# Holding back two weight transfers behind matrix-unit work in the late steps of an attention, router and feed-forward kernel

## The chip, the cores and the metric

The kernel runs on one core of a Trainium2 chip. A core has five engines with a queue of instructions each: PE (matrix products; PEld is its loading of the stationary operand), DVE, ACT, POOL, and SP, which here does nothing but issue DMA transfers, one after the other in the order in which the program wrote them. Sixteen DMA engines move the bytes of every transfer. The metric is the time of one execution in microseconds (us). All of the times below are of the whole kernel unless a stretch is named.

## The reference

Three layers follow each other, all in 32-bit floats (the third's weights come as 64-bit floats in memory and are narrowed in the kernel where they do).

```python
# 1: attention, 4 batches x 8 heads x 576 positions x 64, a causal window of 64
scores = where(0 <= i - j < 64, q @ k.T / 8, -1e9)
attn = softmax(scores)
x = (attn @ v) reshaped to 2304 x 512
# 2: soft mixture of 8 experts with 4 slots each
logits = x @ phi                                # 2304 x 32
slot_input = softmax(logits, over tokens).T @ x # 32 x 512
slot_out[e] = relu(slot_input[e] @ w1[e]) @ w2[e]  # w1: 8 x 512 x 1024, w2: 8 x 1024 x 512
x = softmax(logits, over slots) @ slot_out      # 2304 x 512
# 3: feed-forward
h = x @ w_in                                    # 512 x 2048
out = (h * sigmoid(1.702 h)) @ w_out            # 2048 x 512
```

## The kernel before

**Stages.** Attention comes first, in 18 steps (`for i in range(ns)`): 16 units (a batch and two heads, positions 0 to 511) and 2 steps for the last 64 positions of all batches. The steps overlap: step i does the scores of unit i (`emit_s`, L313 and L328), the turning of the probabilities of unit i-1 (`emit_t`, L348), the turning of the finished rows of unit i-2 (`xt_step`, four 128x128 transposes as PE products, L401), and the product with v of unit i-1 (`emit_pv`, L363). The router's work is spread over the steps. Behind the loop come a short tail of attention and router, then the first expert layer (`emit_w1`, L792), the second (`emit_w2`, L834, and its last pieces, L901), and from about 141 us on the third layer, which is one dense run of PE products (L1014 and L1046).

**Transfers.** The two expert weights are 16 slices of w1 and 16 of w2, of 1 MB each (`plan`). `load_w(n)` takes the next n slices off the plan and writes their transfers into SP's queue (L146). `W_AT` says how many at which step: one at each of the steps 2 to 11, 13 and 14, two at 15, two at 16, three at 17; the rest come behind the loop, as places in SBUF come free (`wslot`, and `dslot` in the attention's own memory, `arena`). Beside them stand the loads of q and k (`load_qk`, L226, of the last positions L228) and of v (`load_v`, L240), written 2 or 3 steps ahead of their use. `AHEAD` (steps 10 to 15) puts a step's slices between its `load_qk` and its `load_v`; otherwise they stand behind both.

**What sets the order.** Each engine does its instructions in the order of the program. A transfer in SP's queue has to wait for its own conditions, and all behind it wait with it: for the reader of the old contents of its place, and for one of eight semaphores that the transfers use in turn (so a transfer waits for the landing of the eighth before it). The slices that the change touches have numbers 10 (step 13), and 14 and 15, the last two of w1 (step 16). Slices 16 to 18, the first three of w2, are those of step 17. The first reader of slices 14 and 15 is the last round of `emit_w1`.

Of the kernel before, what the change touches and what calls it, by code (L numbers as in the profile page):

```python
# [31 lines left out]
HALVES = (slice(0, 256), slice(256, 512))  # L32
LAST_CUT = (slice(0, 384), slice(384, 512))
PIECES = (slice(0, 2), slice(2, 3), slice(3, 4))
W_AT = {**{i: 1 for i in range(2, 17)}, 12: 0, 15: 2, 16: 2, 17: 3}
L_AT = 12
AHEAD = range(10, 16)

# [31 lines left out]
def attention_softmoe_ffn(  # L70
# [12 lines left out]
    nc = tc.nc  # L83
# [21 lines left out]
    def bank(tag, shape=(128, 512), dtype=F32):  # L105
        ring = rings[tag]
        ring.append(ring.pop(0))
        return psp.tile(list(shape), dtype, tag=f"b{ring[-1]}", name=tag)

    ident = cst.tile([128, 128], F32, name="ident")  # L110
# [14 lines left out]
    def wslot(dtype=F32):  # L125
        return wp.tile([128, 4, 512], dtype, tag="w", name="w")

    def dslot(i):
        return mem(2048 * i, 2048).rearrange("p (a f) -> p a f", a=4)
# [3 lines left out]
    plan += [(w2t, w2, i, i if i < 7 else None) for i in range(16)]  # L133
    plan.reverse()

    def load_w(n=1):
        for _ in range(n):
            if plan:
                lst, src, i, d = plan.pop()
                t = wslot() if d is None else dslot(d)  # L140
                v = src[i].rearrange("p (a f) -> p a f", a=4)
                if not plan:
                    t, v = [x.rearrange("p a f -> p (a f)").rearrange(
                        "p (c a f) -> p c a f", c=4, a=4) for x in (t, v)]
                for c in PIECES if not plan else (slice(0, 4),):
                    nc.sync.dma_start(out=t[:, c], in_=v[:, c])  # L146
                lst.append(t)


# [92 lines left out]
    def set_ones(n):  # L242
        v = vbuf(n)
        nc.gpsimd.memset(bass.AP(v.tensor, v.offset, [v.ap[0], [129, 5]]), 1.0)
# [58 lines left out]
    def emit_s(i):  # L303
        u, t = work[i]
        st = [bank("m" if i == 1 and h else "s", (128, 4, 128)) for h in range(2)]
        rows = [slice(64 * h, 64 * h + 64) for h in range(2)]
        for h in range(2):
            for j in range(2):
                o = st[h][rows[j]]
                m = mask[rows[h], j]  # L310
                if t is not None:
                    m = mask[rows[h], 0, 1:2].to_broadcast([64, 4, 128])
                nc.tensor.matmul(  # L313
                    o, identb[rows[h], rows[h]], m,
                    start=True, stop=False, tile_position=(64 * h, 64 * j))
        for c in range(4):
            for h in range(2):
                for j in range(2):
                    r = rows[h]
                    if t is None:  # L320
                        b = qbuf(u)[r]
                        q = b[:, 64 * (2 * c + j):64 * (2 * c + j) + 64]
                        o = c - 1 if c and not j else c
                        k = two(b, 512 + 64 * c, 768 + 64 * o)
                    else:
                        b = qbuf(NU + 2 * t + j)[r, 192 * c:192 * c + 192]
                        q, k = b[:, 0:64], b[:, 64:192]
                    nc.tensor.matmul(  # L328
                        st[h][rows[j], c, :], q, k, start=False, stop=(c == 3),
                        tile_position=(64 * h, 64 * j))  # L330
        nm = sp.tile([128, 2, 4], F32, tag="nm", name="nm")
        for h in range(2):
            nc.vector.tensor_reduce(  # L333
                out=nm[:, h], in_=st[h], axis=AX.X, op=ALU.max, negate=True)
        est[i] = st, nm

    def emit_e(i, h):
        st, nm = est[i]
        for c in range(4):
            nc.scalar.activation(  # L340
                out=pb[h][:, c, :], in_=st[h][:, c, :], func=ACTF.Exp,
                bias=nm[:, h, c:c + 1], scale=1.0)

    def emit_t(i):
        for h in range(2):
            tt = bank("m", (128, 4, 128))
            for c in range(4):
                nc.tensor.transpose(tt[:, c, :], pb[h][:, c, :], ident)  # L348
            nc.scalar.copy(ab[h], tt)  # L349
# [37 lines left out]
    run = {"m": None, "s": None, "acc": None}  # L387

    def xt_step(i, split=False):
        u, t = work[i]  # L390
        pt = bank("m")
        ps = [pt[:, c] for c in HALVES]
        if split:
            ps[1] = bank("m")[:, HALVES[0]]
        for k in range(4):
            if t is None:
                b, kk = divmod(u, NHP)
                src = xb[b % 2][:, k, kk * 128:kk * 128 + 128]
            else:
                src = xl[:, t, k * 128:k * 128 + 128]  # L400
            nc.tensor.transpose(ps[k // 2][:, 128 * (k % 2):128 * (k % 2) + 128], src, ident)  # L401

        def evac():
            if t is None:
                nc.scalar.copy(xT[:, kk], pt)
                return
            o = xlT[:, :, 128 * t:128 * t + 128]
            if not split:
                nc.scalar.copy(o, pt.rearrange("p (k n) -> p k n", k=KD))
                return  # L410
            for k, copy in ((0, nc.scalar.copy), (2, nc.vector.tensor_copy)):
                copy(o[:, k:k + 2], ps[k // 2].rearrange("p (k n) -> p k n", k=2))
        return evac
# [156 lines left out]
    for b in range(B):  # L570
        g = routing(b)
        logits, lmax, dexp, turn, total, slots, gather, norm, side = g
        n = NHP * b
# [25 lines left out]
    def convert(i, first):  # L599
        if not wide:  # L600
            return
        for k in range(5):
            n = CONV_AT.get(i - k)
            if n is None:
                continue
            if k > 1 and first:
                narrow_b(early_raw(n), early_dst(n), (k - 2,))
            elif k == 0 and not first:
                narrow_a(early_raw(n), early_dst(n))
            elif k == 1 and not first:  # L610
                narrow_c(early_dst(n), nc.gpsimd)

    for i in range(ns):
        if i != 2:
            emit_s(i)
        if i:
            emit_t(i - 1)
        for f in lgt.get(i, ()):
            f()
        for f in mid.get(i, ()):  # L620
            f()
        emit_e(i, 0)
        for f in post2.get(i, ()):
            f()
        convert(i, True)
        if i > 1:
            xt_step(i - 2)()
        for f in early.get(i, ()):
            f()
        if i == 1:  # L630
            scale_q(2, nc.vector)
            emit_s(2)
        if i:
            emit_pv(i - 1)
        emit_e(i, 1)
        for f in late.get(i, ()):
            f()
        if i:
            emit_norm(i - 1)
        for f in post.get(i, ()):  # L640
            f()
        if i == 0:
            make_i4()
        if i == 1:
            nc.vector.tensor_copy(
                phi4.rearrange("p k (j s) -> p k j s", j=4),
                phis.unsqueeze(2).to_broadcast([128, KD, 4, NS]))
        if 1 < i < NU - 1:
            scale_q(i + 1, nc.gpsimd)
        for n in {NU - 3: (NU,), NU - 1: (NU + 1,), NU: (NU + 2, NU + 3)}.get(i, ()):  # L650
            scale_q(n, nc.gpsimd)
        if 0 < i < NU:
            set_ones(i)
            shift_v(i)
        elif i >= NU:
            for n in range(2):
                set_ones(NU + 2 * (i - NU) + n)
        if i == L_AT:
            load_qk(NU)
            load_v(NU)  # L660
        if i < NU:
            load_qk(i + 3 + (i + 3 >= NU))
        if i in AHEAD:
            load_w(W_AT.get(i, 0))
        if i < NU + 1:
            load_v(i + 2 + (i + 2 >= NU))
        if i < 2:
            for n in range(2 * i + 2, min(2 * i + 4, FP + N_WO)):
                early_load(n)
        convert(i, False)  # L670
        if i not in AHEAD:
            load_w(W_AT.get(i, 0))

    rings.update(s=[0, 1], t=[2, 7], v=rings["v"])
    cts[0] = s1.tile([128, 1536], F32R, tag="pa", name="cT")
# [7 lines left out]
        out=ml[:, 128:160], in_=pm[0:1, 0:128].rearrange("p (t s) -> p s t", t=TM), axis=AX.X,  # L683
# [12 lines left out]
    def tail_logits(t):  # L696
# [9 lines left out]
    xt = xt_step(ns - 1, True)  # L706
    nc.vector.tensor_scalar(
        out=mm[:, 2:3], in0=pm[:, 0:1], scalar1=-1.0, scalar2=None, op0=ALU.mult)
# [15 lines left out]
        out=ltt, in_=lpt, func=ACTF.Exp, bias=m, scale=1.0, accum_out=ss)  # L724
# [14 lines left out]
    for c in range(2):  # L739
# [9 lines left out]
        out=rsl, in0=pm[:, 0:1], scalar1=ss, scalar2=1e-9, op0=ALU.add, op1=ALU.add)  # L749
# [3 lines left out]
        out=i4s, in0=i4m[:, 0:NS], scalar1=rsl, scalar2=None, op0=ALU.mult)  # L753
    nc.vector.scalar_tensor_tensor(
        out=acc, in0=psl, scalar=al, in1=acc, op0=ALU.mult, op1=ALU.add)
# [479 lines left out]
```

## Time and profile before

| | |
|---|---|
| runs | 362.8, 363.66, 367.47 us; median 363.66 |
| the profiled execution | 362.31 us, its span 360.5 us |
| PE | busy 351.4 us, 97% of the span |
| DVE, ACT, POOL | 67%, 54%, 13% |
| DMA | 70.87 MB, mean 197 GB/s over the span |
| TensorE's granted clock | 1.00 throughout |

The span is cut into 40 slices of 9 us in the page's second part: a digit there is the busy share of an engine, or of the sixteen DMA engines, in tenths. The chain is the row of work that ended last, followed back from the last instruction. "Issue" is time in which an engine waited for nothing that the profile shows. A transfer has two times: the time of its issue on SP, and from there to landing.

### The profile page before, as it was taken

The page shows a single profiled execution, that of the slowest core. Times are in us where ns is not written, and L with a number is a line of the kernel's source. Part 1 is how long each engine was busy: PE and PEld are TensorE (multiplying, and loading weights), DVE is VectorE, ACT ScalarE, POOL GpSimd, SP SyncE. Part 2 cuts the span into 40 slices and gives each one's busy share as a digit, 9 for nine tenths or more (in the row PEclk, how much of TensorE's full clock was granted, in tenths as well). Part 3 has the DMA queues.
Part 4 walks back from the last instruction along what each step waited for, and adds up shares of the span by engine and source line. Part 5 has one row for each costly group of instructions (what it writes and reads, how often), then busy time and mean ns, then how long its engine had stood idle before and what let it go on. Part 6 is the DMA issues. An engine that isn't in the chain of part 4 may idle for free.

```text
span 360.5 us, 7741 instructions
## 1 busy us (share of the span) xinstructions
PE 351.4 (97%) x3021; PEld 269.9 (75%) x3021; DVE 240.5 (67%) x527; ACT 195.6 (54%) x499; POOL 45.5 (13%) x90
## 2 busy tenths in 40 slices
PE   7999999998999999999999999999999999999995
PEld 6787787776634357888788887788886888888884
DVE  4666797976626228885867695988687876262624
ACT  2898899777314026765657444554455453333330
POOL 4366764630100000000000000000000000000000
PEclk9999999999999999999999999999999999999999
DMA  7999999999999994233131313140300000040404
GB/s 278 407 414 405 409 407 413 402 404 407 418 418 422 418 402 150 101 121 113 60 116 58 119 57 119 32 137 9 116 2 0 0 2 1 0 176 0 175 2 175
DMA packets 18180, 70.87 MB, mean 197 GB/s; under 512 B 2016, under 2 KB 2400, under 8 KB 14176
## 3 DMA queue, kind: packets, MB, share of 16 engines
q1 hardware_dynamic: 18000, 70.18, 50.3%
q8 instruction: 24, 0.39, 0.4%
q10 hardware_dynamic: 144, 0.20, 0.2%
q14 instruction: 12, 0.10, 0.1%
HBM read 65.65 MB, written 4.72 MB: 195 GB/s over the span
## 4 chain that ended last, share of the span: by engine, by line
PE 86%; DMA 9%; ACT 2%; issue 1%; DVE 1%; DVEq 0%; ACTq 0%
PE s L1046 18%; PE t L1046 18%; PE v L1046 18%; DMA w<-in_w_dram 8%; PE v L363 5%; PE m L1014 5%; PE m L348 5%; PE s L328 4%; PE s L313 2%; PE m L401 2%; ACT pa L340 2%; PE m L442 1%; PE m L492 1%; DMA rawt<-in_qk_dram 1%; PE m L928 1%
## 5 line engine op out<-in xcount | busy, mean ns | idle before, releaser
L1002 ACT ACTIVATE r<-m 128x384 fp32r<-128x384 f32 (+1 forms) x97 | 47.4, 491 | 80.6 <-PE m L1014 80.5
L1027 DVE TENSOR_TENSOR r<-g,r 128x384 fp32r<-128x384 f32 x96 | 51.4, 554 | 48.4 <-ACT g L1002 40.0
L1046 PE MATMUL t<-w,r 128*128 128x512 f32 x288 | 75.8, 395 | 0.0
L1046 PE MATMUL s<-w,r 128*128 128x512 f32 x288 | 74.3, 392 | 0.0
L1046 PE MATMUL v<-w,r 128*128 128x512 f32 (+2 forms) x291 | 73.4, 387 | 0.0
L1046 PEld LDWEIGHTS t<-w,r 128*128 128x128 f32 x288 | 53.8, 188 | 14.8 <-issue 4.0
L1046 PEld LDWEIGHTS v<-w,r 128*128 128x128 f32 x291 | 54.5, 188 | 11.3
L1046 PEld LDWEIGHTS s<-w,r 128*128 128x128 f32 x288 | 52.6, 188 | 8.5
L1002 ACT ACTIVATE g<-m 128x384 f32<-128x384 f32 x96 | 47.8, 499 | 0.0
L340 ACT ACTIVATE pa<-s,nm 128x128 f32<-128x128 f32 x140 | 41.0, 404 | 5.6 <-DVE nm L333 5.6
L333 DVE TENSOR_REDUCE nm<-s 128x4 f32<-128x512 f32 x35 | 22.5, 684 | 5.5 <-PE s L328 4.8
L1014 PE MATMUL m<-cT,w 128*128 128x384 f32 (+2 forms) x113 | 25.9, 320 | 0.0
L1014 PEld LDWEIGHTS m<-cT,w 128*128 128x128 f32 x113 | 20.8, 188 | 4.9 <-ACT g L1002 0.7
L348 PE MATMUL m<-ident,pa 128*128 128x128 f32 x144 | 20.9, 283 | 0.8 <-ACT pa L340 0.4
L348 PEld LDWEIGHTS m<-ident,pa 128*128 128x128 f32 x144 | 15.6, 140 | 5.0 <-PE s L328 1.7
L349 ACT COPY pa<-m 128x512 f32<-128x512 f32 x18 | 10.7, 596 | 10.2 <-PE m L348 10.2
L982 ACT CAST w<-wf 128x512 fp32r<-128x512 f32 x15 | 9.3, 623 | 9.3 <-DVE wf L176 9.3
L792 PE MATMUL s<-w,phis 128*32 128x512 f32 x128 | 14.1, 594 | 0.0
L382 DVE TENSOR_TENSOR arena<-v,rs 128x256 f32<-128x256 f32 x36 | 13.6, 420 | 0.6
L328 PE MATMUL s<-arena 64*64 64x128 f32 x352 | 13.8, 271 | 0.1
L985 DVE TENSOR_TENSOR w<-wf,w 128x512 fp32r<-128x512 f32 x15 | 10.3, 689 | 5.2 <-ACT w L982 4.9
L1066 DVE TENSOR_TENSOR w<-s,w 128x512 f32<-128x512 f32 x18 | 11.6, 684 | 2.8 <-PE s L1046 2.8
(218 smaller groups left out, 453.3 us busy)
## 6 DMA issues: line engine op xcount, KB each, us to landing
w<-in_w_dram SPq DMA_DIRECT2D x24, 1024.0 KB, 9.9
w<-in_w_out_dram SPq DMA_DIRECT2D x16, 512.0 KB, 3.4
arena<-in_w_dram SPq DMA_DIRECT2D x7, 1024.0 KB, 11.4
iraw<-in_w_in_dram SPq DMA_DIRECT2D x12, 512.0 KB, 3.3
arena<-in_qk_dram SPq DMA_DIRECT2D x10, 512.0 KB, 8.8
out_dram<-w SPq DMA_DIRECT2D x16, 256.0 KB, 2.1
arena<-in_vt_dram SPq DMA_DIRECT2D x13, 258.5 KB, 7.3
rawt<-in_qk_dram SPq DMA_DIRECT2D x6, 512.0 KB, 8.7
```

The source lines that it names most:

```text
L328: nc.tensor.matmul(st[h][rows[j], c, :], q, k, start=False, stop=(c == 3), tile_position=(64 * h, 64 * j))
L333: nc.vector.tensor_reduce(out=nm[:, h], in_=st[h], axis=AX.X, op=ALU.max, negate=True)
L340: nc.scalar.activation(out=pb[h][:, c, :], in_=st[h][:, c, :], func=ACTF.Exp, bias=nm[:, h, c:c + 1], scale=1.0)
L348: nc.tensor.transpose(tt[:, c, :], pb[h][:, c, :], ident)
L363: nc.tensor.matmul(pvt[i][h][64 * j:64 * j + 64, c, :], ab[h][:, c, 64 * j:64 * j + 64], v, start=True, stop=True, tile_position=(0, 64 * j))
L382: nc.vector.tensor_tensor(out=o, in0=pv[h][:, :, 1 - h:65 - h], in1=rs[:, h].unsqueeze(2).to_broadcast([128, 4, 64]), op=ALU.mult)
L792: nc.tensor.matmul(ph[32 * j:32 * j + 32, :], siT[:, kk, :], w1t[4 * r + kk][:, j, :], start=(kk == 0), stop=(kk == KD - 1), tile_position ...
L1002: nc.scalar.activation(out=(gh, g)[part][:, a:e], in_=ph[:, a:e], func=ACTF.Gelu_apprx_sigmoid)
L1014: nc.tensor.matmul(ph[:, c - a:e - a], mst[:, f * 128:f * 128 + 128], cT(c, e - c), start=True, stop=True)
L1027: nc.vector.tensor_tensor(out=gl, in0=g, in1=gh.bitcast(F32), op=ALU.subtract)
L1046: nc.tensor.matmul(accs[t][:, h], a[:, c], b[:, h], start=(first and k == 0), stop=(last and k == 2 and h.stop == 512))
L1066: nc.vector.tensor_tensor(out=o[:, h], in0=accs[t][:, h], in1=o[:, h], op=ALU.add)
```

## The change

Three things are changed, all of them in the transfers of weight slices. `xt_step` keeps its last transposing product in `run["xt"]`. In the steps named in `BEHIND` (13 and 17) `load_w` gets that product and gives the first transfer that it issues a wait for it (`add_manual_dep`). And `W_AT` moves the two slices of step 16 to step 17, which now issues five.

```diff
-W_AT = {**{i: 1 for i in range(2, 17)}, 12: 0, 15: 2, 16: 2, 17: 3}
+W_AT = {**{i: 1 for i in range(2, 17)}, 12: 0, 15: 2, 16: 0, 17: 5}
+BEHIND = (13, 17)
...
+    behind = {}
+
+    def start_w(out, in_):
+        x = nc.sync.dma_start(out=out, in_=in_)
+        if behind:
+            tc.add_manual_dep(x.ins, behind.pop("pe").ins.name, mybir.DependencyInfo(
+                mybir.DependencyClass.Sync, mybir.DependencyReason.DATA), reason="behind")
+
-    def load_w(n=1):
+    def load_w(n=1, pe=None):
+        if pe is not None:
+            behind["pe"] = pe
...
-                    nc.sync.dma_start(out=t[:, c], in_=v[:, c])
+                    start_w(out=t[:, c], in_=v[:, c])
...
-            nc.tensor.transpose(ps[k // 2][:, 128 * (k % 2):128 * (k % 2) + 128], src, ident)
+            run["xt"] = nc.tensor.transpose(
+                ps[k // 2][:, 128 * (k % 2):128 * (k % 2) + 128], src, ident)
...
         if i in AHEAD:
-            load_w(W_AT.get(i, 0))
+            load_w(W_AT.get(i, 0), run["xt"] if i in BEHIND else None)
...
         if i not in AHEAD:
-            load_w(W_AT.get(i, 0))
+            load_w(W_AT.get(i, 0), run["xt"] if i in BEHIND else None)
```

SP's queue around step 13, before the change (behind each transfer the semaphores that it waits for; DMAHW0 to 7 are the eight of the transfers):

```order
L226 DMA rawt<-in_qk_dram 128x1024 [waits DMAHW7_49,PE_49,Pool_49]
L240 DMA arena<-in_vt_dram 128x517 [waits DMAHW0_49,PE_49,Pool_49]
L228 DMA arena<-in_sq_dram 128x768 [waits DMAHW1_49,PE_49,Pool_49]
L146 DMA w<-in_w_dram 128x2048 [waits DMAHW2_49]
L240 DMA rawt<-in_vt_dram 128x517 [waits DMAHW3_49,PE_49,Pool_49]
```

and with the change:

```order
L237 DMA rawt<-in_qk_dram 128x1024 [waits DMAHW7_49,PE_49,Pool_49]
L251 DMA arena<-in_vt_dram 128x517 [waits DMAHW0_49,PE_49,Pool_49]
L239 DMA arena<-in_sq_dram 128x768 [waits DMAHW1_49,PE_49,Pool_49]
L140 DMA w<-in_w_dram 128x2048 [waits DMAHW2_49,PE_49]
L251 DMA rawt<-in_vt_dram 128x517 [waits DMAHW3_49,PE_49,Pool_49]
```

Nothing changes its place; the slice in the fourth row waits for PE now.

SP's queue from the two slices of step 15 to the three of step 17, before the change (the last two transfers of v are those of the steps 15 and 16):

```order
L146 DMA w<-in_w_dram 128x2048 [waits DMAHW0_49]
L146 DMA w<-in_w_dram 128x2048 [waits DMAHW1_49,DVE_49,Activation_49]
L240 DMA arena<-in_vt_dram 128x517 [waits DMAHW2_49,PE_49,Pool_49]
L240 DMA rawt<-in_vt_dram 128x517 [waits DMAHW3_49,PE_49,Pool_49]
L146 DMA w<-in_w_dram 128x2048 [waits DMAHW4_49,DVE_49,Activation_49]
L146 DMA w<-in_w_dram 128x2048 [waits DMAHW5_49,DVE_49,Activation_49]
L146 DMA arena<-in_w_dram 128x2048 [waits DMAHW6_49]
L146 DMA arena<-in_w_dram 128x2048 [waits DMAHW7_49,PE_49,Pool_49]
L146 DMA arena<-in_w_dram 128x2048 [waits DMAHW0_49,PE_49,Activation_49]
```

and with the change:

```order
L140 DMA w<-in_w_dram 128x2048 [waits DMAHW0_49]
L140 DMA w<-in_w_dram 128x2048 [waits DMAHW1_49,DVE_49,Activation_49]
L251 DMA arena<-in_vt_dram 128x517 [waits DMAHW2_49,PE_49,Pool_49]
L251 DMA rawt<-in_vt_dram 128x517 [waits DMAHW3_49,PE_49,Pool_49]
L140 DMA w<-in_w_dram 128x2048 [waits DVE_49,DMAHW4_49,PE_49,Activation_49]
L140 DMA w<-in_w_dram 128x2048 [waits DMAHW5_49,DVE_49,Activation_49]
L140 DMA arena<-in_w_dram 128x2048 [waits DMAHW6_49]
L140 DMA arena<-in_w_dram 128x2048 [waits DMAHW7_49,Pool_49]
L140 DMA arena<-in_w_dram 128x2048 [waits DMAHW0_49,PE_49,Activation_49]
```

Here too the order stays: step 16 wrote nothing into SP's queue behind its two slices. The fifth row (slice 14) waits for PE now, and the eighth (slice 17) no longer does, since the fifth ahead of it has waited for a later point of PE. PE, DVE, ACT and POOL have the same instructions in the same order.

## Rows read from the trace of the kernel before

**Rows 1.** The page's second part: DMA share in tenths and GB/s, 40 slices.

```profile
DMA  7999999999999994233131313140300000040404
GB/s 278 407 414 405 409 407 413 402 404 407 418 418 422 418 402 150 101 121 113 60 116 58 119 57 119 32 137 9 116 2 0 0 2 1 0 176 0 175 2 175
```

**Rows 2.** Busy time by stretch: engines, then clock, DMA share, GB/s.

```profile
84.00:88.00 4.00, 4.00 (x79) 3.23 (x79) 2.57 (x12) 4.00 (x13) 0.21 (x2) 1.00 1.02 416
88.00:131.00 43.00, 40.88 (x409) 18.46 (x408) 18.59 (x53) 10.90 (x26) 1.83 (x1) 1.00 1.01 416
131.00:138.00 7.00, 6.88 (x47) 4.84 (x40) 4.71 (x11) 4.58 (x12) 0.00 (x0) 1.00 0.91 349
141.00:355.00 214.00, 214.00 (x978) 175.32 (x977) 147.81 (x269) 107.25 (x241) 0.00 (x0) 1.00 0.19 65
```

**Rows 3.** The chain that ended last: start, us, what.

```profile
88.67 1.16 issue
...
99.58 2.76 PE s L792 x24
...
102.35 13.34 DMA w<-in_w_dram
...
115.71 15.08 DMA w<-in_w_dram
...
130.84 0.43 PE v L901 x8
```

**Rows 4.** SP in order of time: start of issue, us, transfer.

```profile
63.02 0.33 SPq L228 DMA_DIRECT2D arena<-in_sq_dram  x1
63.39 0.43 SPq L146 DMA_DIRECT2D w<-in_w_dram  x1
65.49 0.33 SPq L240 DMA_DIRECT2D rawt<-in_vt_dram  x1
...
80.47 0.33 SPq L240 DMA_DIRECT2D rawt<-in_vt_dram  x1
80.91 0.85 SPq L146 DMA_DIRECT2D w<-in_w_dram  x2
81.80 15.31 SPq L146 DMA_DIRECT2D arena<-in_w_dram  x7
100.63 15.40 SPq L146 DMA_DIRECT2D w<-in_w_dram  x11
```

**Rows 5.** DMA issues between 80.4 and 81.3: KB, us to landing.

```profile
w<-in_w_dram SPq DMA_DIRECT2D x1, 1024.0 KB, 7.3
rawt<-in_vt_dram SPq DMA_DIRECT2D x1, 258.5 KB, 5.2
```

**Rows 6.** DMA issues between 62.9 and 63.3.

```profile
arena<-in_sq_dram SPq DMA_DIRECT2D x1, 384.0 KB, 7.9
```

**Rows 7.** Transfers of 512 KB at 136 to 165, on L151: count, last line all seven.

```profile
L151 SPq DMA_DIRECT2D iraw<-in_w_in_dram x4: 327/327/328, 152.3 to 164.2; - x4
L151 SPq DMA_DIRECT2D w<-in_w_out_dram x3: 327/328/328, 136.6 to 147.2; - x3
...
DMA to landing us min/median/max: 3.1/3.3/3.7
```

**Rows 8.** PE in step 17, in order of time.

```profile
83.50 0.60 PE L401 MATMUL m<-ident,arena 128*128 128x128 f32 x4
84.03 0.69 PE L363 MATMUL v<-arena,pa 128*64 128x65 f32 x15
```

**Rows 9.** PE in step 13, in order of time.

```profile
61.81 1.04 PE L328 MATMUL s<-arena 64*64 64x128 f32 x32
...
63.71 0.60 PE L401 MATMUL m<-ident,arena 128*128 128x128 f32 x4
...
64.75 0.64 PE L363 MATMUL v<-rawt,pl 128*64 128x65 f32 x16
```

## The prediction

> **What bounds the kernel now.** I read the page's slices first, then the busy times by stretch, then the chain, and last SP's queue with the landings.
>
> The slices show two kernels in one [rows 1]. For the first 15 slices of 9 us, up to about 135 us, the DMA engines are busy to nine tenths or more (the first slice apart) and move some 410 GB/s; after that they are mostly idle. The stretches say the same more sharply [rows 2]: from 88 to 131 us the DMA share is 1.01 at 416 GB/s, from 141 to 355 us it is 0.19 and PE is busy 214.00 of 214 us. PE is also nearly always busy before 131 us, but that is no bound there, and the chain shows why [rows 3]: behind 2.76 us of the first expert layer it runs through two transfers of weight slices, 13.34 us from 102.35 and 15.08 us from 115.71, and only at 130.8 us is PE on it again. So two stages decide: **a stream of transfers that ends at 130.8 us, and then PE**. What delays the stream's last byte delays all behind it by as much, since PE from 141 us on has no idle time to give back [rows 2].
>
> The stream is a queue. Transfers land in the order of their issue, and each waits for those ahead. The v load of 80.47 us needs 5.2 us to land at 85.7, and the slice of 80.91 us needs 7.3 and lands at 88.2 [rows 4, 5]: 2.5 us later, which is what 1 MB takes at 416 GB/s (1.049 MB / 416 = 2.52 us). A transfer's late issue therefore costs nothing as long as its predecessors still keep the DMA engines busy when its own first bytes are ready.
>
> **Step 13.** One slice waits newly for the transposes of `xt_step`. They end at 63.71 + 0.60 = 64.31 us [rows 9]; SP issued the slice at 63.39 [rows 4]. What SP needs from a PE end to an issue I take from the rows: the scores end at 62.85 and the q and k load that waits for them goes at 63.02, 0.17 us; the product with v ends at 65.39 and its load goes at 65.49, 0.10 us [rows 4, 9]. So the slice goes at about 64.45, 1.05 us later. Cover: the transfer just ahead, issued at 63.02, lands 7.9 us later, at 70.9 [rows 4, 6], so 6.5 us of queue still stand before the slice. Cost 0. Behind the slice in SP's queue stands the v load, which goes at 65.49 because of PE [rows 4]; the slice's issue takes 0.43 us, so SP is free again at 64.9 and the load is not late. Cost 0.
>
> **Step 17.** Slices 14 and 15 went at 80.91 and, right behind it, 81.4; slice 16, first of the step's own three, at 81.80 [rows 4]. Now slice 14 waits for the transposes, which end at 83.50 + 0.60 = 84.10 [rows 8]. With 0.10 to 0.17 us for SP it goes at 84.2, **3.3 us later**. The four behind it follow at SP's pace, 0.85 us for two [rows 4], so about 84.7, 85.1 and 85.6, each late by 3 us or so; slice 18 waited for PE's later work anyway. No load of q, k or v stands behind them, so attention itself waits for nothing new, and no engine's instructions move.
>
> What covers 3.3 us? Ahead of slice 14 the queue lands its last transfer at 85.7 [rows 4, 5], 1.5 us after the new issue. This is the thinnest cover in the stream, and a transfer doesn't start at once. How long one takes with nothing ahead is seen later, where the DMA engines idle [rows 7]: seven transfers of 512 KB take 3.1 to 3.7 us from issue to landing, median 3.3. Another 512 KB at 416 GB/s add 1.26 us, so 1 MB needs 4.4 to 5.0 us, at the median 4.6. Slice 14 would land at 84.2 + 4.6 = 88.8 us against 88.2 before: **0.6 us later**, with 0.4 and 0.9 from the ends of the row. Slices 15 to 17 are in the queue within 1.4 us and follow without a gap, so from there the stream is as dense as before and all of it is 0.6 us late. The bound below is 0, if the 1.5 us of queue hide the whole start; the bound above is the whole 3.3 us, if nothing of it is hidden. I take 0.6, since its rows are the same kind of transfer on the same queue.
>
> Does anything between take the 0.6 us back? SP's next pause, in which the places of w1 come free, ends at 100.63; eleven slices and pieces go from there [rows 4]. Before it, slice 15 and the seven of 81.80 were issued [rows 4], and eight slices behind a landing at 88.2 reach to 88.2 + 8 x 2.52 = 108.4 us: 7.7 us of queue are left. There is no gap to fill either: 1.01 of DMA share up to 131 and 0.91 from 131 to 138 us [rows 2]. PE reads slices 14 and 15 in the last round of `emit_w1`, after 99.58 [rows 3], some 9 us behind their landing (88.2 and 2.5 more). So nothing is given back, and nothing is lost besides.
>
> **Sum.** 362.31 us (the profiled execution, 360.5 of span and 1.8 around it) + 0 + 0.6 = 362.9 us. The three timed runs have their median at 363.66, 1.35 above the profiled one; the middle of all four executions is (362.8 + 363.66) / 2 = 363.2. On that I forecast 363.2 + 0.6 = **363.8 us**.
>
> **Rivals.**
>
> *A, no gap.* The start of slice 14 is fully hidden behind the 1.5 us of queue. For it: of the starts at 63.02 and 80.47 us nothing is seen in the landings. Against it: those transfers landed 7.9 and 5.2 us after their issue [rows 5, 6], so they stood in a longer queue. Time 363.2. If slice 14 lands within 0.2 us of 88.2, it was this.
>
> *B, slower by the whole delay.* A landing tells only of the last of sixteen DMA engines. If most of them are through with the queue soon after 80.9 us, they stand idle until slice 14 comes, and what they lose is lost to the stream: 84.2 - 80.9 = 3.3 us at most, 366.5 us. It decides as soon as the DMA share between 82 and 87 us falls well below 1 and the landings after it are late by more than 1 us. For it: no row tells how much of the queue is left on each engine. Against it: slice 14 lands just its own 2.5 us behind the v load [rows 5], so the engine that is last sets the pace, and that one has 1.5 us of work left at 84.2. [...]
>
> *C, a gain.* With fewer transfers in the queue, something that the stream shares with attention gets through sooner: the chain has an idle 1.16 us at 88.67 with no releaser [rows 3]. But attention's end is not on the path: SP's wait for it at 100.63 ends with 7.7 us of queue in hand. A gain must come from the rate itself. The slices reach 422 GB/s at their best [rows 1]; if all 43 us from 88 to 131 ran at that instead of 416, it would save 43 x 6 / 422 = 0.6 us: 362.6. No row says why it should.
>
> *D, the change waits longer than it says.* If SP's new wait ended only with a later PE product, each further us would be a us of gap; I see no reason in rows, and leave it in the upper end.
>
> **How the numbers follow.** Forecast 0.65, A 0.17, B (anything from 1 us to 3.3 us, with D) 0.13, C 0.05. The range reaches from 362.2 (C, or A on a run like the fastest) to 365.8 (B short of its full price); what is left out is the rest of B and an execution like the 367.47 one. Two per cent, about what a measurement of this kernel can tell from no change, is 7.3 us. B's full price is 3.3 us, under half of that, and the largest gain is a tenth of it; so faster by over 2% 0.01, within 2% 0.97, slower by over 2% 0.02.
>
> **What would show it.** In the changed kernel: SP issues the slice of step 13 near 64.4 us and the first of step 17 near 84.2, the transfers around step 13 land as before, slice 14 lands near 88.8 us, a dip of the DMA share stands between 82 and 87 us, and the last piece of w2 lands at 131.4 us instead of 130.8, the rest of the program moved by the same amount. It is wrong if the end of the stream moves by more than 1 us or comes earlier, or if PE's stretch from 141 us on changes in length.

## The result and the profile after

The changed kernel takes 365.5 us (median of 22 runs, 364.15 to 370.54), the kernel before 362.89 in the same comparison (22 runs, 362.28 to 367.47): a ratio of 1.0061, with the interval from 1.0033 to 1.0090. The ratio is taken over the fast runs, without the two of the changed kernel at 370.31 and 370.54 us, and is not the quotient of these medians (1.0072). So the change is slower by about 2.2 us (1.2 to 3.3). That is no change by the 2% bound, inside the range, and on the side that the forecast named, but the forecast's own term was 0.6 us. The profiled execution takes 364.8 us with a span of 363.0, 2.5 us over the span before.

The page's slices of the changed kernel, to be set beside [rows 1]: DMA share in tenths, and GB/s.

```profile
DMA  7999999997999995333130403031300000040404
GB/s 289 409 412 403 412 409 411 404 391 292 421 418 421 418 405 201 117 116 116 58 116 11 165 32 143 3 133 40 116 2 0 0 2 1 0 174 1 174 2 173
```

One slice of the stream stands out, the tenth (82 to 91 us): 292 GB/s where [rows 1] have 407. Behind it the slices are much as before up to the sixteenth, in which the changed kernel still moves 201 GB/s for 150.

The busy times by stretch of the changed kernel (five engines, granted clock, DMA share, GB/s), which answer to [rows 2], with the 8 us around the place of the change ahead:

```profile
80.00:88.00 8.00, 7.82 (x153) 6.44 (x148) 5.62 (x21) 7.06 (x25) 0.23 (x3) 1.00 0.71 268
...
84.00:88.00 4.00, 4.00 (x81) 3.37 (x79) 2.78 (x12) 4.00 (x14) 0.21 (x2) 1.00 0.59 209
88.00:131.00 43.00, 39.64 (x368) 17.29 (x370) 18.14 (x53) 11.32 (x27) 1.83 (x1) 1.00 1.01 418
131.00:138.00 7.00, 6.48 (x78) 3.84 (x70) 2.96 (x9) 2.20 (x7) 0.00 (x0) 1.00 1.03 407
141.00:355.00 214.00, 214.00 (x977) 175.12 (x976) 148.05 (x270) 108.88 (x245) 0.00 (x0) 1.00 0.19 66
```

The same 8 us of the kernel before:

```profile
80.00:88.00 8.00, 7.82 (x140) 6.15 (x137) 5.45 (x20) 7.06 (x23) 0.21 (x2) 1.00 1.02 408
```

PE is as busy in both, 7.82 us; the transfers are not. Idle DMA time is (1 - 0.71) x 8 = 2.3 us against none before, and the missing bytes, (408 - 268) x 8 / 416, are worth 2.7 us of stream. From 88 us on the rate is the old one (418 against 416), and from 141 us on PE has its 214.00 us as before. The chain of waits of the changed kernel (start, us, what) carries the loss to the end, compare [rows 3]:

```profile
88.46 1.10 PE v L374 x32
...
98.63 2.76 PE s L804 x24
101.41 16.82 DMA w<-in_w_dram
118.24 15.08 DMA w<-in_w_dram
```

The last weight piece lands at 118.24 + 15.08 = 133.32 us, before at 115.71 + 15.08 = 130.79: 2.5 us later, which is the whole difference of these two spans. The execution of before that was profiled is among its fastest, though, so one pair of traces doesn't settle the size; the timed runs give the 2.2 us. Attention itself ends a little earlier (98.63 against 99.58, and the idle 1.16 us of [rows 3] is gone), and gains nothing by it: the chain goes straight into a longer wait for weights, 16.82 us instead of 13.34.

SP in order of time in the changed kernel, beside [rows 4], and under it the row of SP's waits on the moved slice's new condition (total us, times, longest):

```profile
63.44 0.33 SPq L239 DMA_DIRECT2D arena<-in_sq_dram  x1
64.76 0.33 SPq L140 DMA_DIRECT2D w<-in_w_dram  x1
65.89 0.33 SPq L251 DMA_DIRECT2D rawt<-in_vt_dram  x1
...
80.89 0.33 SPq L251 DMA_DIRECT2D rawt<-in_vt_dram  x1
84.60 0.80 SPq L140 DMA_DIRECT2D w<-in_w_dram  x2
85.45 10.72 SPq L140 DMA_DIRECT2D arena<-in_w_dram  x7
```

```profile
SPq L140 <- PE m L412: 3.2, 1, 3.2
```

PE at the two places in the changed kernel, beside [rows 8, 9]:

```profile
64.13 0.60 PE L412 MATMUL m<-ident,arena 128*128 128x128 f32 x4
...
83.92 0.60 PE L412 MATMUL m<-ident,arena 128*128 128x128 f32 x4
```

And the DMA issues from 80.8 to 84.7 us in the changed kernel (KB, us to landing), beside [rows 5]:

```profile
w<-in_w_dram SPq DMA_DIRECT2D x1, 1024.0 KB, 5.4
rawt<-in_vt_dram SPq DMA_DIRECT2D x1, 258.5 KB, 4.8
```

The waits resolve where the change puts them: the transposes end at 84.52, slice 14 goes at 84.60. It lands at 84.60 + 5.4 = 90.0 us, 1.8 us later than before. The v load ahead lands at 80.89 + 4.8 = 85.7, exactly as before. If the landings are all that one reads, 1.1 us of queue stand before the slice when it is issued. What the sixteen engines really did shows in half-microsecond stretches of the changed kernel (same columns as above):

```profile
82.50:83.00 0.50, 0.50 (x19) 0.33 (x8) 0.02 (x1) 0.29 (x2) 0.00 (x0) 1.00 1.03 400
83.00:83.50 0.50, 0.50 (x6) 0.50 (x6) 0.50 (x1) 0.00 (x0) 0.00 (x0) 1.00 0.55 210
83.50:84.00 0.50, 0.50 (x7) 0.50 (x6) 0.50 (x2) 0.26 (x1) 0.00 (x0) 1.00 0.24 91
84.00:84.50 0.50, 0.50 (x6) 0.33 (x4) 0.47 (x3) 0.50 (x2) 0.00 (x0) 1.00 0.27 103
84.50:85.00 0.50, 0.50 (x18) 0.50 (x19) 0.43 (x3) 0.50 (x3) 0.00 (x0) 1.00 0.17 62
85.00:85.50 0.50, 0.50 (x23) 0.50 (x18) 0.36 (x2) 0.50 (x4) 0.11 (x1) 1.00 0.18 45
85.50:86.00 0.50, 0.50 (x21) 0.43 (x21) 0.26 (x2) 0.50 (x3) 0.11 (x1) 1.00 0.54 98
86.00:86.50 0.50, 0.50 (x24) 0.31 (x16) 0.47 (x3) 0.50 (x3) 0.00 (x0) 1.00 0.55 131
86.50:87.00 0.50, 0.50 (x10) 0.30 (x9) 0.39 (x2) 0.50 (x4) 0.00 (x0) 1.00 1.02 393
```

From 83.5 us on three quarters of the DMA engines' time is idle, a microsecond before the slice is issued and two before the v load lands. Counted packet by packet in the trace, 16 or more are under way at any moment from 82.5 to 83.0 us, and four to seven, on the mean under five, from 83.5 to 84.5. So about a third of the engines or fewer still carried that load. The rate is back 1.9 us after the issue, from 86.5 on.

### The profile page after: what moved, and what is told of

Its sections match the earlier page's. It is cut to its first block, busy times and chain, and to the rows that moved or that the text cites. A ratio compares the mean times of both kernels' runs of the same rounds, so it can differ in the third digit from the quotient of the medians.

```text
span 363.0 us, 7743 instructions
## 1 busy us (share of the span) xinstructions
PE 352.1 (97%) x3021; PEld 269.9 (74%) x3021; DVE 240.6 (66%) x527; ACT 195.6 (54%) x499; POOL 44.6 (12%) x90
## 4 chain that ended last, share of the span: by engine, by line
PE 85%; DMA 10%; ACT 2%; DVE 1%; issue 1%; DVEq 0%; ACTq 0%
PE s L1058 18%; PE t L1058 18%; PE v L1058 18%; DMA w<-in_w_dram 9%; PE v L374 5%; PE m L1026 5%; PE m L359 5%; PE s L339 4%; PE s L324 2%; PE m L412 2%; ACT pa L351 1%; PE m L454 1%; PE m L504 1%; DMA rawt<-in_qk_dram 1%; PE m L940 1%; PE s L804 1%
## 6 DMA issues: line engine op xcount, KB each, us to landing
arena<-in_vt_dram SPq DMA_DIRECT2D x13, 258.5 KB, 7.0
```

## The experiments

Two theories were set against each other first: a thin gap (only the start of slice 14 past the last landing is lost, the prediction's own), and rival B (the engines run dry one by one, so most of the delay is lost). A third question came with the trace: slice 16 landed 3.25 us behind slice 15 instead of 2.5, and I took those 0.75 us for a second loss. The expectations speak of landings; the account by idle DMA time, which settles the matter, stands behind the single runs.

**Only step 13 held.**

```diff
-W_AT = {**{i: 1 for i in range(2, 17)}, 12: 0, 15: 2, 16: 0, 17: 5}
-BEHIND = (13, 17)
+W_AT = {**{i: 1 for i in range(2, 17)}, 12: 0, 15: 2, 16: 2, 17: 3}
+BEHIND = (13,)
```

> Only the wait of step 13; step 16 keeps its two slices, step 17 its three, without a wait. Theory G (the loss is a gap in the transfer stream behind the held slice of step 17, since a start into empty queues takes about 5.4 us for 1 MB and only 1.1 us of queue stood before it): slice issued near 64.7, lands as before near 73.5, last piece of w2 at 130.8, ratio 1.000. Rival S13 (the wait of step 13 has a share): stream ends later than 131.3, ratio over 1.002.

Measured: 363.21 us, ratio 1.0019 (0.9984 to 1.0054). The slice went at 65.11 us and landed at 73.22, no later than before (73.49). Step 13 shows no part in the loss. The last weight piece landed at 131.56 us, which the expectation had as a sign of such a part, but the second trace of before, below, has it at 132.94 without any wait.

**Only step 17 held.**

```diff
-BEHIND = (13, 17)
+BEHIND = (17,)
```

> Only the wait of step 17 with its five slices; none at step 13. Theory G: as the whole change, slice 14 lands at 90.0, last piece of w2 near 133.3, ratio 1.006 (1.004 to 1.008). Rival S13: less than 1.004.

Measured: 365.3 us, ratio 1.0059 (1.0034 to 1.0084): all of the loss. Slice 14 went at 85.08 and landed at 90.36.

**Only slice 15 and its followers held**, slice 14 issued at step 16 as before.

```diff
-W_AT = {**{i: 1 for i in range(2, 17)}, 12: 0, 15: 2, 16: 0, 17: 5}
+W_AT = {**{i: 1 for i in range(2, 17)}, 12: 0, 15: 2, 16: 1, 17: 4}
```

> Slice 14 goes at step 16 without a wait, only slices 15 to 18 are held behind the transposes of step 17: 1 MB (2.5 us) more of queue before the held one. Theory G: slice 14 lands at 88.2, slice 15 is issued at 84.2 to 84.6 and would be ready at 89.6 to 90.0, before its turn at 90.7, so no gap: last piece of w2 at 130.8, ratio 1.000 (0.998 to 1.002). Rival B of the prediction (most DMA engines are through with their queue before the last one, and what they stand idle is lost): slices 15 to 18 are still held 3 us, some engines idle, stream 0.5 to 1 us late, ratio 1.0015 to 1.003.

Measured: 363.45 us, ratio 1.0004 (0.9975 to 1.0032). SP in this kernel, and its busy times by stretch:

```profile
81.45 0.33 SPq L251 DMA_DIRECT2D rawt<-in_vt_dram  x1
81.88 3.60 SPq L140 DMA_DIRECT2D w<-in_w_dram  x2
```

```profile
80.00:88.00 8.00, 7.82 (x153) 6.27 (x152) 5.78 (x20) 7.06 (x24) 0.21 (x2) 1.00 1.00 369
```

Slice 15 waited for the same product (it went at 85.15), and no DMA time was idle: with one slice of 1 MB, 2.5 us, more in the queue the same wait costs nothing that these runs show. I read this as speaking against B at the time; it only shows that the cover is what counts. It doesn't decide between the theories: no engine ran dry, so by either little is lost here, and the interval, which reaches 1.2 us, doesn't exclude the 0.5 to 1 us of the expectation.

**Held behind the last score product of step 17, an earlier point.**

```diff
-                    nc.tensor.matmul(
+                    run["sc"] = nc.tensor.matmul(
...
-            load_w(W_AT.get(i, 0), run["xt"] if i in BEHIND else None)
+            load_w(W_AT.get(i, 0), run["sc"] if i in BEHIND else None)
```

> As the change, but at step 17 the five slices wait for the last score product of the step instead of the transposes, which ends 1.5 us earlier (82.6). Slice 14 goes at 82.8 to 83.2. Theory G: ready 5.4 us later, 88.2 to 88.6, against its old landing of 88.2: first slice 0 to 0.4 us late, last piece of w2 130.8 to 131.2, up to 132 if a second delay on one engine follows as in the change (0.75 us between slices 15 and 16); ratio 1.000 to 1.003. Rival B: the delay of 1.9 to 2.3 us is lost to the most part, stream 1.5 us late or more, ratio over 1.004.

Measured: 366.25 us, ratio 1.0066 (1.0024 to 1.0108): missed, it is no better than the change, though the slice went earlier, at 83.86. The stretches of this kernel show a smaller first hole and a second one:

```profile
80.00:88.00 8.00, 7.54 (x151) 6.05 (x150) 5.66 (x19) 6.79 (x23) 0.21 (x2) 1.00 0.89 319
...
92.00:94.00 2.00, 2.00 (x23) 1.93 (x19) 1.12 (x4) 0.00 (x0) 0.00 (x0) 0.62 1.02 430
94.00:96.00 2.00, 2.00 (x10) 1.56 (x8) 0.45 (x2) 0.37 (x1) 0.00 (x0) 0.53 1.01 422
...
98.00:104.00 6.00, 5.40 (x48) 3.38 (x48) 3.58 (x13) 3.31 (x9) 1.83 (x1) 1.00 0.92 365
```

PE stood idle 1.98 us at 89.81 with no releaser, and right behind it the granted clock is 0.62 and 0.53. The slices that wait for attention's late products went at 98.28 us instead of 94.97, and the DMA share fell from 98 to 104 us. The chain goes through PE's first expert layer here and no longer through a transfer, so that attention's late end may cost by itself; how much is not shown:

```profile
102.88 7.00 PE s L804 x64
...
110.97 7.00 PE s L804 x64
```

**The same kernel again**, one execution with its trace.

> The kernel that holds the slices behind the last score product of step 17, a second trace. Theory G: issue at 83.0 to 83.9; if no fetch falls into its start, slice 14 is ready 4.6 to 5.3 us later, at 87.6 to 89.2; in the first trace it was 6.0 us with a fetch of 1.27 us in it. Rival B: 89.0 to 89.9 also without a fetch.

Measured: 366.72 us. PE idle 1.70 us at 90.08, clock 0.60, 0.50, 0.50 and 0.69 in the four stretches from 92 to 100 us, those slices at 99.76. The second hole was not one execution's. Slice 14 went at 84.12 and landed 6.15 us later, past the times of both theories; with a fetch of instructions in it again (one packet of 8 KB and 1.33 us on the queue that the trace names `q14 instruction`), this doesn't test the start without one.

**Held behind the product that ends the first half of those scores**, earlier still.

```diff
-                    nc.tensor.matmul(
+                    mm = nc.tensor.matmul(
...
+                    if c == 1:
+                        run["sc"] = mm
...
-            load_w(W_AT.get(i, 0), run["xt"] if i in BEHIND else None)
+            load_w(W_AT.get(i, 0), run["sc"] if i in BEHIND else None)
```

> As the change, but the five slices of step 17 wait for the product that ends the first half of the step's scores: issue near 82.0 to 82.5, some 1.1 to 1.6 us later than before, when the queue still reaches to 85.6. Theory G (only what the queue does not cover of a start of 4.6 to 5.3 us is lost): ready at 86.6 to 87.8, before its turn at 88.1, so no gap behind the last engine: slice 14 lands within 0.2 us of 88.2, ratio 0.999 to 1.002. Rival B (engines that are through before the last one stand idle, and that is lost): slice 14 lands 0.5 us or more late, DMA share from 80 to 84 us under 0.97, ratio 1.002 to 1.004.

Measured: 366.7 us, ratio 1.0062 (1.0027 to 1.0098). The first hole is nearly closed, as was expected, and the second stays. Its stretches, and the place on its chain:

```profile
80.00:88.00 8.00, 7.82 (x154) 6.27 (x153) 5.87 (x20) 7.06 (x24) 0.22 (x2) 1.00 0.97 357
...
92.00:94.00 2.00, 2.00 (x20) 1.88 (x17) 1.05 (x4) 0.00 (x0) 0.00 (x0) 0.50 0.99 418
...
98.00:104.00 6.00, 5.40 (x48) 3.38 (x48) 3.53 (x12) 3.23 (x9) 1.83 (x1) 1.00 0.97 356
```

```profile
89.73 1.98 issue
```

Slice 14 went at 83.34, later than expected, and landed 2.49 us behind the v load, in turn: the first hole's theory held, and the ratio was missed. The second hole is (422 - 356) x 6 / 416 = 0.95 us by bytes, but only (1 - 0.97) x 6 = 0.2 us by idle DMA time, so what makes up the 2.2 us of this ratio isn't shown. The runs of this kernel and of the last but one spread widely (363.22 to 370.06, and 362.80 to 368.96), so the second hole may be absent from some executions; none of their three traces is one.

**Held behind the last router product of step 17, a later point.**

```diff
-                    nc.tensor.matmul(
+                    run["lg"] = nc.tensor.matmul(
...
-            load_w(W_AT.get(i, 0), run["xt"] if i in BEHIND else None)
+            load_w(W_AT.get(i, 0), run["lg"] if i in BEHIND else None)
```

> As the change, but the five slices of step 17 wait for the last router product of the step, which ends 2.3 us behind the transposes. Theory G (a gap behind the held slice, whose start into empty queues takes 5.3 us): issue near 86.7, slice 14 lands near 92.0 (3.8 us late), last piece of w2 at 134.6 to 135.4, ratio 1.010 to 1.0125. Rival W (it is the wait itself or the order of SP's queue that costs, not the length of the gap): the same as the change, 1.006.

Measured: 369.15 us, ratio 1.0153 (1.0090 to 1.0216). The slice went at 87.22, 2.6 us later than in the change. The ratio lies above the 1.010 to 1.0125 of the expectation, which its interval still holds; the wait or the order alone (1.006 again) is out. By stretch:

```profile
84.00:86.00 2.00, 2.00 (x44) 1.76 (x46) 1.57 (x6) 1.96 (x6) 0.21 (x2) 1.00 0.19 63
86.00:88.00 2.00, 2.00 (x41) 1.62 (x42) 1.26 (x5) 2.00 (x8) 0.00 (x0) 1.00 0.00 0
88.00:92.00 4.00, 3.98 (x54) 3.22 (x52) 2.92 (x14) 2.13 (x7) 0.00 (x0) 1.00 0.97 324
```

Once the engines were dry (share 0.19, then 0.00) a further microsecond of delay cost about one of stream (2.3 us more held than in the change, 2.2 more of missing bytes): those missing from 80 to 92 us are worth (408 - 196) x 8 / 416 + (412 - 324) x 4 / 416 = 4.9 us (before has 412 GB/s from 88 to 92).

**Slice 14 as two transfers of 512 KB.**

```diff
-                for c in PIECES if not plan else (slice(0, 4),):
+                cut = (slice(0, 2), slice(2, 4)) if len(w1t) == 14 and lst is w1t else (slice(0, 4),)
+                for c in PIECES if not plan else cut:
```

> As the change, with slice 14 cut into two transfers of 512 KB. Theory S (a start of 1 MB into empty queues is slow because its packets are 8 KB: 5.3 us, where 512 KB of 4 KB packets take 3.3 us): first half lands 3.3 us after its issue, second 1.3 us later, 4.6 in all, slice 14 near 89.2 instead of 90.0; ratio 1.003 to 1.005. Rival F (the slow start is a fetch of instructions that falls into it): first half takes 4.0 us or more or second half is late, 5.3 us in all, ratio 1.006.

Measured: 365.74 us, ratio 1.0073 (1.0028 to 1.0117). The halves landed 4.3 and 5.6 us after the first issue; the time is the change's. The size of the pieces isn't what costs here.

**Before and change once more**, one execution each.

> The kernel before, unchanged, for a second trace. Theory R1 (the long step of 0.75 us between two landings near 92 to 96 us, behind a fetch of instructions, belongs to the gap): steps of 2.5 us from 88 to 128, last piece of w2 at 130.8. Rival R2 (such a step comes with or without the gap, by which DMA engine is last at that moment): one of 0.4 to 0.8 us here too, last piece at 131.3 to 131.8.

> The change, unchanged, for a second trace. Slice 14 is issued at 84.2 to 84.7 and lands 5.3 to 5.4 us later, a long step of 0.7 to 0.9 us follows the fetch near 92.5, last piece of w2 at 133 to 134.

Measured: 364.45 us for the kernel before, 364.88 for the change. The second trace of before has a long landing step too, 3.6 us between slices 14 and 15, without any hole:

```profile
80.00:88.00 8.00, 7.54 (x152) 6.01 (x150) 6.06 (x20) 6.78 (x22) 0.27 (x4) 1.00 1.00 363
```

So such a step doesn't belong to the change. Nor is the one in the change a second loss: the rate from 92 to 98 us is 421 GB/s, as before, with the DMA share at 1.01. The landings only show the first loss late, 1.8 us of it at slice 14 and 2.5 from slice 16 on. The second trace of the change missed its expectation in part: slice 14 took 5.74 us to land, not 5.3 to 5.4, and its step to slice 16 is 0.4 us too long, not 0.7 to 0.9.

The row above holds a warning too. At a share of 1.00 that execution moved (408 - 363) x 8 / 416 = 0.9 us less of stream than the first of before: the packets took longer (those of 8 KB 341 ns on the mean, for 320), with no engine idle. Its stream ended 2.15 us later than the first one's, though nothing was held; 0.4 us of that is idle DMA time from 76 to 80 us, at a share of 0.89. A single trace's bytes and landings thus vary by nearly as much as the change costs; what separates the kernels is the idle time at the place of the change. Without a hole the stream ended at 130.79, 131.56 (only step 13), 131.80 (only slice 15) and 132.94 us, against 133.32 to 133.83 in the four traces held at the transposes.

**All later by a start-up delay.** To see whether the phase between attention and stream matters, 60 one-column products were put ahead of attention, with the change and without it.

```diff
+    tiny = bank("v")
+    for _ in range(60):
+        nc.tensor.matmul(tiny[:, 0:1], pa[:, 0:128], pa[:, 0:1], start=True, stop=True)
```

> As the change, with 60 products of one column more on PE at the very start, where it waits for its first transfer; they write to a bank that nothing reads. They move the places in PE's program at which its instructions are fetched (each fetch is a 16 KB packet of about 1.05 us on one DMA engine) by about half a period. Theory R (0.75 us of the change's loss is the fetch at 92.2, which falls on a DMA engine that has no lead any more after the gap): fetches near 82 to 83 and 89 to 90; the long step between two landings moves from slice 16 (95.7) to slice 14 or 15 or is gone, and slice 14 takes less than 5.2 us from issue if the fetch at 85.5 was part of its slow start. Rival Q (slice 16 is late because its own issue on SP took 1.5 us): the long step stays between slices 15 and 16. Ratio 1.003 to 1.007.

> The kernel before with the same 60 small products. Theory R: without a gap the DMA engines keep different leads, fetches cost nothing or what they cost before; ratio 0.998 to 1.003, stream end within 1 us of 130.8 to 131.8. If the small products themselves cost something, it shows here.

Measured: 392.2 us (ratio 1.0785) with the change and 388.75 (1.0673) without, far from the expectations, since the products held PE for over 22 us. The whole times are no clean pair: there are four runs of each, and the mean granted clock was 0.994 in the one trace and 0.965 in the other. But the place of the change can be compared, some 26 us later than before. The v load ahead of slice 14 goes at 106.53 us with the change and at 106.76 without; slice 14 goes 4.30 and 0.43 us behind it. The stretch around it, first with the change, then without:

```profile
105.00:120.00 15.00, 14.08 (x224) 10.95 (x222) 10.84 (x41) 9.77 (x32) 0.21 (x2) 1.00 0.81 310
105.00:120.00 15.00, 13.13 (x215) 10.73 (x214) 9.84 (x37) 9.83 (x31) 0.21 (x2) 1.00 1.00 400
```

That is 2.9 us of idle DMA time against none, and the last weight piece lands at 159.70 against 156.75 us. So the loss comes with the hole at this phase too. The long landing step of the change stays between slices 15 and 16 (3.33 us), as rival Q had it; without the change one stands between slices 14 and 15 (3.23 us).

**The account over all traces.** Idle DMA time between 80 and 88 us is (1 - share) x 8, from the row of that stretch in each trace; "held" is the issue of slice 14 less that of the v load ahead of it. A share over 1 gives a number just below zero, which means none.

| kernel | held, us | share, GB/s | idle, us | ratio, or one time |
|---|---|---|---|---|
| before | 0.44 | 1.02, 408 | -0.2 | |
| before, again | 0.43 | 1.00, 363 | 0.0 | 364.45 us |
| only step 13 | 0.43 | 1.01, 392 | -0.1 | 1.0019 |
| only slice 15 | 0.43 | 1.00, 369 | 0.0 | 1.0004 |
| first half of scores | 1.81 | 0.97, 357 | 0.2 | 1.0062, second hole |
| last score | 2.52 | 0.89, 319 | 0.9 | 1.0066, second hole |
| last score, again | 2.24 | 0.93, 333 | 0.6 | 366.72 us, second hole |
| the change | 3.71 | 0.71, 268 | 2.3 | 1.0061 |
| the change, again | 3.69 | 0.74, 268 | 2.1 | 364.88 us |
| halves | 3.68 | 0.71, 249 | 2.3 | 1.0073 |
| only step 17 | 3.98 | 0.70, 254 | 2.4 | 1.0059 |
| last router product | 6.02 | 0.51, 196 | 3.9 | 1.0153 |

Idle time is what is held less 1.4 to 1.7 us in the kernels from 1.8 to 4 us, 2.1 in the last. The four that are held at the transposes have 2.1 to 2.4 us of it, which is what the timed runs show for the change, 2.2. The pair with the products fits as well (held 4.30, idle 2.9). The kernels with a second hole don't: their ratios are the change's at 0.2 to 0.9 us of idle time here, and what else they lose is open.

## Why the prediction was right in sign and wrong in size

**What bounds.** Right: the stream up to its last piece, then PE, whose 214.00 us from 141 us on didn't change; the 2.5 us of the stream's end arrive whole at the end.

**Step 13.** Right, cost 0: the slice went at 64.76 (64.45 forecast, and attention ran 0.42 us later here) and landed at 73.63, against 73.49. The v load behind it went at 65.89, on PE's own time, and was not held up.

**Step 17, the issue.** Right: 84.60 us for 84.2, the 0.42 us being attention's again, and the four behind it at SP's pace. The v load is later by the same 0.42, so what the change adds is 3.71 - 0.44 = 3.27 us, as forecast.

**Step 17, the cover. This is the step that failed.** The prediction took the landing of the v load for the end of the queue's work: "Ahead of slice 14 the queue lands its last transfer at 85.7 [rows 4, 5], 1.5 us after the new issue". That is the end of the last engine. Most of the others were through by 83.5, as the share of 0.24 from 83.5 to 84.0 us shows, so little work was left when the slice was issued. With the start counted, held time less idle time leaves 1.4 us of cover behind the v load's issue (3.71 - 2.3); 0.44 us of that were used before the change too. So about 1.0 of the added 3.27 us was hidden, not 2.7. By its own sign, "if the end of the stream moves by more than 1 us", the prediction was wrong here: it moved by 2.5.

The trace has sixteen updates of the semaphore for the landing of each of its 126 transfers, as many as there are DMA engines, and for the v load they come one by one: in the changed kernel from 83.31 to 85.70 us, ten of them by 83.77, in the kernel before from 82.99 to 85.70. The landing at 85.7 is the last of the sixteen.

**Step 17, the start.** The forecast had 4.6 us for 1 MB into an empty queue, from transfers of 512 KB that stood alone; the slice took 5.4, and over the kernels with a hole or near one 5.2 to 6.2. In the forecast's sum of landings this is 0.8 of the 1.8 us by which slice 14 was late (0.6 forecast), and attention's 0.42 the other part that it lacked. That too is a number of the last engine: fifteen of the slice's sixteen updates come from 89.15 to 89.35 us, the last at 89.99. For the stream what counted is when the rate was back, 1.9 us after the issue, and the 2.1 us of start that the forecast contains (4.6 - 2.52) were sound.

**Afterwards.** Right: nothing is given back between 88 and 131 us (418 against 416 GB/s), and no second gap stands there.

**The rivals.** B is the one that holds, with some seven tenths of its price (2.3 us of idle time out of 3.3): its test was a DMA share well below 1 between 82 and 87 us and landings late by over 1 us, and the trace falls to 0.24 and lower, and is 1.8 us late. I had given it 0.13, on the argument that the last engine sets the pace. That argument is the mistake, and the range held the time only because part of B's price was in it: 365.5 us stands near its upper end, 365.8, and far from the forecast of 363.8. A is out. C's observation was true, the idle 1.16 us went away, and its worth nothing, as the chain shows. D is out, SP goes 0.08 us after the product.

## What to carry to other kernels

Here holding a transfer back left no DMA time idle while the queue still had work on all DMA engines (a share of 1.00 with one slice more ahead, 0.71 in the change), and a landing told of the slowest one (ten of the v load's sixteen updates came 1.9 us or more before its last): read the DMA share in stretches of half a microsecond, or leave a whole transfer more in the queue than the landings ask for (2.5 us more were enough here). Price a loss of a stream by the idle DMA time over a stretch, and in more than one trace: single landing steps moved by 0.4 to 1.1 us with no engine idle, and the bytes of the same 8 us by 0.9 us between two traces of one kernel. Where a wait is moved to an earlier point, look again at what else the new transfers meet.

## What the runs showed of the hardware that was not expected

- The end of the queue was ragged: in the changed kernel the DMA share falls from 1.03 to 0.24 within a microsecond, and the last 258.5 KB transfer lands 2 us after that.
- PE has an idle time with no releaser in the last product with v of step 17: 1.16 us before, 1.43 in the second trace of before and with step 13 alone, 1.70 to 1.98 with the earlier points of waiting, none in the change. In these six traces a fetch of instructions on the DMA engines (16 KB, on the queue that the trace names `q8 instruction`) ends at 88.5 to 90.5 us, and PE goes on 1.2 to 1.4 us after it; in the six without idle time it ends at 86.6 to 87.5. The execution before has 24 such packets, 1.06 us each on the mean, for 6042 products and weight loads of PE, one for 252, and with the change they end at the same places of PE's program, to within 35 of the 3131 instructions of its sequencer. That a late fetch holds PE up, and that the slices delay it, is argued from these times, and no run takes it away alone.
- After 1.98, 1.98 and 1.70 us of that idle time the granted clock fell to 0.50 to 0.75 over the two to four stretches of 2 us from 92 us on; after 1.16 and 1.43 us it stayed at 1.00 in three traces.
